# A fixed bound on the deviation, checked by a running minimum, in an attention and squared-ReLU MLP kernel

## The chip, the cores and the metric

The kernel runs on one core of a Trainium2 chip. The metric is the time of one execution on the device in microseconds (us), lower is better. The engines of the core work side by side, each on its own queue in order: TensorE (PE; its weight loads are PEld), VectorE (DVE), ScalarE (ACT), GpSimd (POOL) and SyncE (SP), which issues the DMA transfers.

## The reference

For each of four batches of 12480 tokens with 128 channels, 32 inducing points attend to the tokens, which gives h (32 x 128); then the tokens attend to h; the result goes through an MLP with 2048 hidden columns and a squared ReLU.

```python
def mab(q, kv):
    s = scale * (q @ kv.transpose(0, 2, 1))
    s = s - s.max(-1, keepdims=True)
    a = np.exp(s)
    a /= a.sum(-1, keepdims=True) + 1e-09
    return a @ kv
h = mab(I, x)                 # I: 32 inducing points, x: (4, 12480, 128)
y = mab(x, h).reshape(-1, 128)
hid = y @ w_in                # w_in 128 x 2048, w_out 2048 x 128
return np.maximum(hid, 0.0) ** 2 @ w_out
```

## The kernel before

**Data.** x comes twice: transposed as xT (128 channels on the partitions) and as it is, xn. Both weight matrices come as 64-bit floats and are narrowed to 32 bits on VectorE (`narrow`, lines 199 to 212, tiles named ni, no; seven instructions for each of eight pieces of 128 x 512). A batch has 26 chunks of 480 tokens, in seven groups G: six of four chunks and one of two. A group of xT (`xp`, 128 x 1920 f32, 960 KB) serves as many as three readers: the first scores, the maximum described below, and the second scores. Nine such buffers exist. xn is loaded in 14 pieces per batch (`xnb`, five buffers).

**Stages of a batch b.**

- `first(b)`: scores of the inducing points (s, line 236), moved to sT with their maxima (line 254); the overall maximum (mx, m, gm, nb); exponentials on ScalarE (line 300); transposes (en, line 310); h is summed on TensorE from en and xnb (hacc, line 323) and from group to group on VectorE (hq, line 331); scaled and transposed it is hn and hT.
- `prepare(b)`: because the attention of a token over the 32 points of h is nearly uniform, the MLP is expanded about the mean. hwv = h times w_in (line 448). From the largest and smallest entry of each hidden column (hi_c, lo_c) and a bound rho on the relative deviation follows whether the column is always positive, always dead, or mixed. Positive columns are folded into products of pairs of inducing points (G, line 605; wq, line 611; w16), mixed ones, at most 16, get slots of their own. The bound: `largest(G)` in `first` (line 292) takes the largest absolute value of each channel over the tokens of a group (`xm`), 28 reductions in all; `prepare` multiplies it by the largest deviation of h from its mean (dh) on TensorE and gets rho with the maximum row.
- `second(b, G)`: the second scores (s, line 236, with hT), transposed to e, softmax over the 32 points (lines 364 to 375, on VectorE, GpSimd and ScalarE), transposed back (a32), and written as a high and a low 16-bit half of a - 1/32, scaled by 2^14 (a16: line 385 on ScalarE or 387 on VectorE, then the rest at line 388 on VectorE). It goes to DRAM (ad, line 389) and comes back transposed (dT, line 409, `load_dT`).
- `squares(b, G)`: the mixed slots and the rest of the singles (sq, z, zz, back into dT, lines 422 to 434).
- Chunks: `up` makes hp from dT and a constant `pairs` (line 639), `lift` squares it on ScalarE (g, line 648), `down` sums po (lines 654, 655), which is moved to o with scale and bias (line 658 on ScalarE or 660 on VectorE) and stored.

**Order.** `background(k)` deals out the steps of `second`, `squares`, and of `first` and `prepare` of the next batch beside the chunks, so many by each half chunk. `to_act` sends a movable copy (outputs, a16, w16) to whichever of ScalarE and VectorE has less in the running sums `held`, to which every larger step adds its estimated time. The tile context is opened with `schedule_with_timeline_sim=True`: when the program is built, a simulated timeline sets the order of the instructions on every engine, so an edit moves others too.

**Proof at the end.** For each batch `flags` holds whether the mixed columns fit in 16 slots, whether rho is at most 2^-8, and whether the scales fit. Their minimum is read into a register; where it is 0, a second, full path over all columns (`every_column`) runs for all batches.

Of the kernel before, what the change touches and what calls it, by code (L numbers as in the profile page):

```python
# [31 lines left out]
RHO_MAX = 2.0 ** -8  # L32
# [8 lines left out]
def attend_then_relu2_mlp(ctx: ExitStack, tc: tile.TileContext, xn, xT, indT, w_in, w_out, outT):  # L41
# [78 lines left out]
    flags = const.tile([1, NB], F32, name="flags")  # L120
# [119 lines left out]
    def first(b):  # L240
# [49 lines left out]
        def largest(G):  # L290
            held["dve"] += 60 + 1.042 * 4 * WID[G]
            nc.vector.tensor_reduce(  # L292
                st.xm[:, G:G + 1], st.xp[G], axis=AX.X, op=ALU.max, apply_absolute_value=True,
            )

# [11 lines left out]
        for G, nb32 in enumerate(BLK):  # L307
# [7 lines left out]
            largest(G)  # L315
# [121 lines left out]
    def prepare(b):  # L437
# [44 lines left out]
        nc.tensor.matmul(ps[:, 0:2], ones, row, start=True, stop=True)  # L482
        two = small("two", 2)
        nc.vector.tensor_copy(two, ps[:, 0:2])
        rho = two[:, 1:2]
# [15 lines left out]
        ts(omr, rho, -1.0, 1.0, op0=ALU.mult, op1=ALU.add)  # L501
# [438 lines left out]
```

## Time and profile before

| | us |
|---|---|
| three runs: median (lowest to highest) | 562.29 (556.12 to 562.49) |
| the profiled execution | 565.03 |
| its span from first to last instruction | 563.2 |

| engine | busy us | share of the span |
|---|---|---|
| TensorE | 422.6 | 75% |
| VectorE | 365.6 | 65% |
| ScalarE | 294.4 | 52% |
| GpSimd | 82.2 | 15% |

The profile page gives, for one execution, the busy time of each engine, the span in 40 slices of 14.1 us with a digit for the busy tenths, the clock granted to TensorE in tenths, and the share of the 16 DMA engines. A group of instructions (line, engine, operation, result<-operands, count) has its busy time, the mean of one in ns, and behind the bar the idle time before it and who ended it. The chain of work that ended last is followed back from the last instruction, at each step to what released it. HBM reads are 64.91 MB and writes 31.95 MB over the span.

### The profile page before, as it was taken

To read this page: it belongs to the slowest core of one execution; us is meant where nothing else is said; L and a number is where in the kernel's file an instruction comes from. 1 tells how busy PE (TensorE), PEld (TensorE's weight loads), DVE (VectorE), ACT (ScalarE), POOL (GpSimd) and SP (SyncE) were. 2 spreads that over 40 slices of the span, in tenths; PEclk is the share of its full clock that TensorE was granted. 3 is DMA by queue.
4 is the path that set the end of the run, shared out by engine and by line. 5 is a ranking of instruction groups with operands and counts; after the bars stand their busy time and mean duration, and the time that the engine had idled before them with its cause. 6 is when DMAs were issued, how large, how long until landed. Compare 5 with 4: busy or idle time off the path is not lost.

```text
span 563.2 us, 8828 instructions
## 1 busy us (share of the span) xinstructions
PE 422.6 (75%) x3083; PEld 202.7 (36%) x3083; DVE 365.6 (65%) x947; ACT 294.4 (52%) x419; POOL 82.2 (15%) x93
## 2 busy tenths in 40 slices
PE   1635355986778988869789889779779989669792
PEld 0023334622233535522244536423234555223340
DVE  8999768466382674675574384986653377787541
ACT  0030113338395794334687883426486875357771
POOL 0000011021120110122211010132121021234200
PEclk9999557699697998776899988878898999898987
DMA  8998313126559863253778943263567312244642
GB/s 317 410 358 310 132 70 118 41 80 212 140 160 345 292 216 115 72 169 107 216 237 294 334 167 115 76 227 115 174 216 264 128 54 72 90 151 133 203 150 82
DMA packets 64591, 100.83 MB, mean 179 GB/s; under 512 B 22800, under 2 KB 53776, under 8 KB 64528
## 3 DMA queue, kind: packets, MB, share of 16 engines
q1 hardware_dynamic: 64528, 100.08, 52.9%
q8 instruction: 28, 0.46, 0.4%
q14 instruction: 35, 0.29, 0.2%
HBM read 64.91 MB, written 31.95 MB: 172 GB/s over the span
## 4 chain that ended last, share of the span: by engine, by line
PE 39%; DMA 24%; DVE 22%; ACT 5%; SPq 4%; issue 3%; POOL 0%; ACTq 0%; DVEq 0%; POOLq 0%
PE hp L639 11%; DMA dT<-ad 7%; PE po L654 6%; PE s L236 6%; DMA xp_False<-xT_dram 6%; DMA ad<-a 5%; DVE xm L292 5%; ACT g L648 4%; DMA xnb<-xn_dram 3%; PE wq L611 3%; DVE G L605 3%; PE hwv L448 3%; PE hacc L323 2%; SPq L409 2%; DMA outT_dram<-o 2%
## 5 line engine op out<-in xcount | busy, mean ns | idle before, releaser
L648 ACT ACTIVATE g<-hp 128x960 f16<-128x960 f32 x208 | 193.5, 972 | 105.0 <-PE hp L639 92.8
L639 PE MATMUL hp<-dT,pairs 96*128 96x480 f16 x416 | 129.3, 407 | 16.2 <-ACT g L648 9.6
L654 PE MATMUL po<-g,w 128*128 128x480 f16 x416 | 114.7, 381 | 13.0 <-DVE o L660 5.1
L639 PEld LDWEIGHTS <-pairs 96*128 96x128 f16 x416 | 36.8, 104 | 84.4 <-issue 60.2
L368 POOL TENSOR_TENSOR e<-e,mx 128x480 f32<-128x480 f32 (+1 forms) x28 | 27.0, 965 | 261.5 <-DVE mx L364 208.2
L654 PEld LDWEIGHTS <-w 128*128 128x128 f16 x416 | 40.9, 102 | 63.6 <-issue 24.6
L292 DVE TENSOR_REDUCE xm<-xp_False 128x1 f32<-128x1920 f32 (+1 forms) x28 | 55.9, 1999 | 8.4 <-DMA xp_False<-xT_dram 8.3
L658 ACT ACTIVATE o<-po,bias,osc 128x480 f32<-128x480 f32 x66 | 48.7, 757 | 15.6 <-PE po L655 14.7
L236 PE MATMUL s<-xp_False,indT_sb 128*32 128x480 f32 (+1 forms) x224 | 37.4, 756 | 18.3 <-DMA xp_False<-xT_dram 13.3
L323 PE MATMUL hacc<-xnb,en 128*32 128x128 f32 x784 | 35.6, 317 | 19.6 <-DMA xnb<-xn_dram 7.6
L655 PE MATMUL po<-dT,lin 128*128 128x480 f16 x104 | 39.9, 400 | 9.3 <-DMA dT<-zz 9.0
L432 POOL TENSOR_TENSOR zz<-z 128x480 f16<-128x480 f32 (+1 forms) x28 | 27.6, 985 | 111.7 <-DVE z L428 87.9
L660 DVE TENSOR_SCALAR o<-po,osc,bias 128x480 f32<-128x480 f32 x38 | 28.8, 763 | 18.4 <-PE po L655 13.7
L375 POOL TENSOR_TENSOR e<-e,z 128x480 f32<-128x480 f32 (+1 forms) x28 | 26.9, 961 | 87.8 <-DVE z L374 67.6
L323 PEld LDWEIGHTS hacc<-xnb,en 128*32 128x32 f32 x784 | 25.5, 125 | 32.5 <-issue 15.7
L300 ACT ACTIVATE sT<-sT,nb 128x480 f32<-128x480 f32 (+1 forms) x28 | 18.3, 657 | 35.2 <-DVE nb L287 35.2
L362 DVE STREAM_TRANSPOSE e<-s 128x480 f32<-128x480 f32 (+1 forms) x28 | 18.0, 644 | 25.6 <-PE s L236 25.4
L428 DVE TENSOR_SCALAR z<-sq,off,cut 128x480 f32<-128x480 f32 (+1 forms) x28 | 21.5, 769 | 18.0 <-PE sq L422 17.5
L236 PE MATMUL s<-xp_False,hT 128*32 128x480 f32 (+1 forms) x224 | 30.0, 610 | 0.1
L605 DVE TENSOR_TENSOR G<-hwp,hw 128x512 f16<-128x512 f16 x64 | 25.9, 460 | 5.6 <-PE wq L611 5.6
L378 DVE STREAM_TRANSPOSE a<-e 128x480 f32<-128x480 f32 (+1 forms) x28 | 17.7, 633 | 13.0 <-POOL e L375 13.0
L422 PE MATMUL sq<-dT,singles 96*32 96x480 f16 x104 | 11.4, 398 | 19.4 <-DMA dT<-ad 18.0
(208 smaller groups left out, 493.3 us busy)
## 6 DMA issues: line engine op xcount, KB each, us to landing
outT_dram<-o SPq DMA_DIRECT2D x104, 240.0 KB, 2.6
xp_False<-xT_dram SPq DMA_DIRECT2D x24, 960.0 KB, 6.3
xnb<-xn_dram SPq DMA_DIRECT2D x28, 448.0 KB, 5.8
xnb<-xn_dram SPq DMA_DIRECT2D x24, 512.0 KB, 6.5
dT<-ad SPq DMA_DIRECT2D x72, 120.0 KB, 2.6
ad<-a SPq DMA_DIRECT2D x24, 240.0 KB, 2.6
dT<-zz SPq DMA_DIRECT2D x104, 30.0 KB, 1.9
wi<-w_in_dram SPq DMA_DIRECT2D x4, 512.0 KB, 5.7
```

The lines of the kernel that those rows point to most:

```text
L236: nc.tensor.matmul(ps[32 * q:32 * q + 32, 0:w], lhsT, xp[:, w * q:w * q + w], start=True, stop=True,)
L292: nc.vector.tensor_reduce(st.xm[:, G:G + 1], st.xp[G], axis=AX.X, op=ALU.max, apply_absolute_value=True,)
L323: st.last = nc.tensor.matmul(hacc[32 * q:32 * q + 32, 0:P], en[:, t], xg[:, t % 8], start=t < 4, stop=t + 4 >= nb32,)
L368: nc.gpsimd.tensor_tensor(e[:, 0:t], e[:, 0:t], mx[:, 0:t].unsqueeze(2).broadcast_to([P, t, MI]), op=ALU.subtract)
L432: nc.gpsimd.tensor_tensor(g[rows], zv[rows], zv[rows], op=ALU.mult)
L605: tt(g[:, :, MI * j:MI * j + n], hwp[:, :, 0:n], hw16f[:, :, s0:s0 + n], op=ALU.mult)
L639: nc.tensor.matmul(hp[:, i, 0:CH].rearrange("p (q t) -> p q t", q=4), pairs[0:96, (2 * j + i) * P:(2 * j + i + 1) * P], self.dT[0:96], sta ...
L648: nc.scalar.activation(self.g[:, 2 * j:2 * j + 2], self.hp.pop(j)[:, 0:2, 0:CH], AF.Square)
L654: nc.tensor.matmul(po[:, 0:CH], st.w16[:, i], self.g[:, i], start=i == 0, stop=False)
L655: nc.tensor.matmul(po[:, 0:CH].rearrange("p (q t) -> p q t", q=4), st.lin, self.dT, start=False, stop=True)
L658: nc.scalar.activation(o, po[:, 0:CH], AF.Identity, bias=st.bias, scale=st.osc)
L660: nc.vector.tensor_scalar(o, po[:, 0:CH], st.osc, st.bias, op0=ALU.mult, op1=ALU.add)
```

## The change

The bound on the deviation is no longer computed from the data but fixed at 2^-10 (RHO) and checked afterwards. `largest`, its tile xm, and the instructions of `prepare` that make rho of it (dh, ah, the product of xm and dh, the second half of row, omr, the second flag) are gone; the columns' classes use the constant. In `second`, a running minimum over all tokens, `least_d` (128 x 480, 16 bits), takes in each high half of a16 just after the low half; `smallest()`, one step behind the last `second`, reduces it, transposes it on TensorE, reduces again and compares it with -0.498, which goes into a fifth flag. Since `largest` no longer adds to `held`, the balance of `to_act` shifts: output evictions on ScalarE and VectorE are 40 and 64 instead of 66 and 38, a16 conversions 13 and 15 instead of 19 and 9, w16 14 and 2 instead of 16 and 0. The simulated timeline then orders every queue anew.

```diff
-RHO_MAX = 2.0 ** -8
+RHO = 2.0 ** -10
+D_MIN = -0.498
...
-    flags = const.tile([1, NB], F32, name="flags")
+    flags = const.tile([1, NB + 1], F32, name="flags")
+    least_d = const.tile([P, CH], F16, name="least_d")
+    nc.vector.memset(least_d, 0.0)
...
-        def largest(G):
-            held["dve"] += 60 + 1.042 * 4 * WID[G]
-            nc.vector.tensor_reduce(
-                st.xm[:, G:G + 1], st.xp[G], axis=AX.X, op=ALU.max, apply_absolute_value=True,
-            )
-
...
             if G + 2 < NG:
                 exp(G + 2)
-            largest(G)
...
         if not again:
+            nc.vector.tensor_tensor(least_d[:, 0:w], least_d[:, 0:w], a16[:, 0, 0:w], op=ALU.min)
             st.aT[G] = load_dT(b, G)
...
-            if h == 0:
-
-                xm, dh, ah = small("xm"), small("dh", MI), small("ah", MI)
-                nc.vector.tensor_reduce(xm, st.xm, axis=AX.X, op=ALU.max)
-                ts(dh, st.hT[:, 0:MI], st.hT[:, P:P + 1], None, op0=ALU.subtract)
-                stt(dh, dh, -1.0, dh, op0=ALU.mult, op1=ALU.max)
-                stt(ah, st.hT[:, 0:MI], -1.0, st.hT[:, 0:MI], op0=ALU.mult, op1=ALU.max)
-                stt(dh, ah, 2.0 ** -18, dh, op0=ALU.mult, op1=ALU.add)
...
-        nc.tensor.matmul(ps[0:1, P:P + MI], xm, dh, start=True, stop=True)
-        row = work.tile([1, 2], F32, tag="row", name=f"row_{b}")
-        nc.vector.tensor_reduce(row[:, 0:1], ps[0:1, 0:P], axis=AX.X, op=ALU.max)
-        nc.vector.tensor_reduce(row[:, 1:2], ps[0:1, P:P + MI], axis=AX.X, op=ALU.max)
-        ts(row[:, 0:1], row[:, 0:1], 2.0 ** -60, None, op0=ALU.max)
-        ts(row[:, 1:2], row[:, 1:2], 2 * scale * (1 + 2.0 ** -8), 2.0 ** -16, op0=ALU.mult, op1=ALU.add)
+        row = work.tile([1, 1], F32, tag="row", name=f"row_{b}")
+        nc.vector.tensor_reduce(row, ps[0:1, 0:P], axis=AX.X, op=ALU.max)
+        ts(row, row, 2.0 ** -60, None, op0=ALU.max)
...
-        ts(vm, v, omr, None, op0=ALU.mult)
-        ts(up, hi, 0.0, rho, op0=ALU.max, op1=ALU.mult)
+        ts(vm, v, 1.0 - RHO, None, op0=ALU.mult)
+        ts(up, hi, 0.0, RHO, op0=ALU.max, op1=ALU.mult)
...
-        ts(fits[:, 0:1], bp[0:1, 2:3], MX + 0.5, None, op0=ALU.is_le)
-        ts(fits[:, 1:2], row[:, 1:2], RHO_MAX, None, op0=ALU.is_le)
-        tt(flags[:, b:b + 1], fits[:, 0:1], fits[:, 1:2], op=ALU.mult)
+        ts(flags[:, b:b + 1], bp[0:1, 2:3], MX + 0.5, None, op0=ALU.is_le)
...
+    def smallest():
+
+        m = small("dmin")
+        nc.vector.tensor_reduce(m, least_d, axis=AX.X, op=ALU.min)
+        tp = att_psum("dmin_t")
+        nc.tensor.transpose(tp[0:1, 0:P], m, ident)
+        t = work.tile([1, 1], F32, tag="dmin1", name="dmin1")
+        nc.vector.tensor_reduce(t, tp[0:1, 0:P], axis=AX.X, op=ALU.min)
+        nc.vector.tensor_scalar(flags[:, NB:NB + 1], t, D_MIN, None, op0=ALU.is_ge)
+        yield
+
+    ahead = chain(*(second(b, G) for b in range(NB) for G in range(NG)), smallest())
```

The line numbers of the kernel after are some lower or higher than before: sT is line 254 before and 256 after, narrow 206 to 212 and 208 to 214, `second`'s lines 362 to 388 become 357 to 383, and line 386 is the new minimum.

The first place is VectorE's queue in the first scores of batch 0, where the scores s are moved to sT between the steps of narrowing w_in (ni) and, before, the maxima (xm). Before:

```order
L254 TENSOR_SCALAR sT_213,mx_215<-s_0_2_238 128x480
L292 TENSOR_REDUCE xm_133<-xp_3_False 128x1
L208 TENSOR_SCALAR ni_m<-ni_a 128x512
L254 TENSOR_SCALAR sT_213,mx_215<-s_0_3_254 128x480
L292 TENSOR_REDUCE xm_133<-xp_4_False 128x1
L254 TENSOR_SCALAR sT_213,mx_215<-s_0_4_260 128x480
L209 SCALAR_TENSOR_TENSOR ni_r<-wi_175,ni_m 128x512
L292 TENSOR_REDUCE xm_133<-xp_5_False 128x1
L292 TENSOR_REDUCE xm_133<-xp_6_False 128x1
L254 TENSOR_SCALAR sT_213,mx_215<-s_0_5_274 128x480
```

After:

```order
L256 TENSOR_SCALAR sT_213,mx_215<-s_0_2_238 128x480
L210 TENSOR_SCALAR ni_m<-ni_a 128x512
L211 SCALAR_TENSOR_TENSOR ni_r<-wi_177,ni_m 128x512
L212 TENSOR_TENSOR ni_r<-ni_a,ni_r 128x512
L213 TENSOR_SCALAR ni_m<-wi_177 128x512
L256 TENSOR_SCALAR sT_213,mx_215<-s_0_3_254 128x480
L214 SCALAR_TENSOR_TENSOR w_in_sb<-ni_m,ni_r 128x512
L256 TENSOR_SCALAR sT_213,mx_215<-s_0_4_260 128x480
L256 TENSOR_SCALAR sT_213,mx_215<-s_0_5_274 128x480
L208 TENSOR_SCALAR no_a<-wo_266 128x512
```

The narrowing has moved up to where the maxima were: the last piece of w_in is done here, and the first of w_out (wo) begins.

The second place is VectorE's queue at the end of batch 0's `first`, from the scaling of h (zr, hn) to hT and the scale of w_out (wo_m). Before:

```order
L338 TENSOR_SCALAR zr<-hs_502 128x1
L212 SCALAR_TENSOR_TENSOR wo_sb<-no_m,no_r 128x512
L207 SCALAR_TENSOR_TENSOR no_a<-wo_272,no_a 128x512
L339 RECIPROCAL zr<-zr 128x1
L686 TENSOR_REDUCE wm_170<-wo_sb 128x1
L208 TENSOR_SCALAR no_m<-no_a 128x512
L340 TENSOR_SCALAR hn_134<-hs_502,zr 128x128
L209 SCALAR_TENSOR_TENSOR no_r<-wo_272,no_m 128x512
L344 COPY hT_155<-ht_508 128x128
L345 TENSOR_REDUCE hT_155<-ht_508 128x1
L210 TENSOR_TENSOR no_r<-no_a,no_r 128x512
L211 TENSOR_SCALAR no_m<-wo_272 128x512
```

After:

```order
L333 TENSOR_SCALAR zr<-hs_495 128x1
L334 RECIPROCAL zr<-zr 128x1
L335 TENSOR_SCALAR hn_135<-hs_495,zr 128x128
L339 COPY hT_155<-ht_501 128x128
L340 TENSOR_REDUCE hT_155<-ht_501 128x1
L187 TENSOR_REDUCE wo_m<-wo_t 1x1
L341 TENSOR_SCALAR hT_155<-hT_155 128x1
L188 TENSOR_SCALAR wo_m<-wo_m 1x1
```

The narrowing of the last piece of w_out (wo_272) now stands ahead of the third group's sum hq, before the last transposes en, and no longer between the small steps.

The third place is VectorE's queue where batch 1 takes over from batch 0: the last products G_1_3 for wq, and the attention weights of batch 1's second group (z2_1_1, a32_1_1, a16_1_1), whose result goes to ad and dT. Before:

```order
L372 TENSOR_REDUCE z2_1_1_2071<-e2_1_1_1971 128x15
L292 TENSOR_REDUCE xm0_133<-xp_2_3_False_2321 128x1
L373 TENSOR_SCALAR z2_1_1_2071<-z2_1_1_2071 128x15
L605 TENSOR_TENSOR G_1_3_2051<-hwp_1_1745,hw16_1_1697 128x16x32 x3
L605 TENSOR_TENSOR G_1_3_2051<-hwp_1_1745,hw16_1_1697 128x16x16
L607 CAST G_1_3_2051<-hwS_1_1740 128x16x16
L613 TENSOR_REDUCE wm5_1918<-wq_1_2_2028 128x1
L374 RECIPROCAL z2_1_1_2071<-z2_1_1_2071 128x15
L378 STREAM_TRANSPOSE a32_1_1_2122<-e2_1_1_1971 128x480
L388 SCALAR_TENSOR_TENSOR a16_1_1_2124<-a32_1_1_2122,lessen_105,a16_1_1_2124 128x480
```

After:

```order
L368 TENSOR_SCALAR z2_1_1_2029<-z2_1_1_2029 128x15
L591 TENSOR_REDUCE wm5_1876<-wq_1_2_1986 128x1
L369 RECIPROCAL z2_1_1_2029<-z2_1_1_2029 128x15
L638 TENSOR_SCALAR o_0_24_2146<-po_0_24_2140,osc0_142,bias0_143 128x480
L373 STREAM_TRANSPOSE a32_1_1_2080<-e2_1_1_1929 128x480
L591 TENSOR_REDUCE wm5_1876<-wq_1_3_2034 128x1
L638 TENSOR_SCALAR o_0_25_2187<-po_0_25_2181,osc0_142,bias0_143 128x480
L594 TENSOR_REDUCE cm2_1826<-wm5_1876 128x1
L383 SCALAR_TENSOR_TENSOR a16_1_1_2082<-a32_1_1_2080,lessen_105,a16_1_1_2082 128x480
L386 TENSOR_TENSOR least_d_133<-least_d_133,a16_1_1_2082 128x480
```

The maximum ahead of z2 is gone; two outputs of batch 0 (o_0_24, o_0_25), which ScalarE moved before, stand between the reciprocal and a16, and the minimum behind it.

More of the change, by code (lines that the diff above doesn't have):

```diff
@@ L127, in attend_then_relu2_mlp @@
         one = Batch()
-        one.xm = const.tile([P, NG], F32, name=f"xm{k}")
         one.hn = const.tile([P, P], F32, name=f"hn{k}")
@@ L473, in prepare @@
         nc.tensor.transpose(ps[0:1, 0:P], am, ident)
-        nc.tensor.matmul(ps[0:1, P:P + MI], xm, dh, start=True, stop=True)
-        row = work.tile([1, 2], F32, tag="row", name=f"row_{b}")
-        nc.vector.tensor_reduce(row[:, 0:1], ps[0:1, 0:P], axis=AX.X, op=ALU.max)
-        nc.vector.tensor_reduce(row[:, 1:2], ps[0:1, P:P + MI], axis=AX.X, op=ALU.max)
-        ts(row[:, 0:1], row[:, 0:1], 2.0 ** -60, None, op0=ALU.max)
-        ts(row[:, 1:2], row[:, 1:2], 2 * scale * (1 + 2.0 ** -8), 2.0 ** -16, op0=ALU.mult, op1=ALU.add)
+        row = work.tile([1, 1], F32, tag="row", name=f"row_{b}")
+        nc.vector.tensor_reduce(row, ps[0:1, 0:P], axis=AX.X, op=ALU.max)
+        ts(row, row, 2.0 ** -60, None, op0=ALU.max)
         yield
         ps = att_psum(f"bc_{b}")
[L482 to L485, printed above, removed]
+        nc.tensor.matmul(ps[:, 0:1], ones, row, start=True, stop=True)
         p2 = small("p2")
-        ts(p2.bitcast(I32), two[:, 0:1].bitcast(I32), 0x7F800000, None, op0=ALU.bitwise_and)
-        mg, nmg, s, k2, omr = small("mg"), small("nmg"), small("s"), small("k2"), small("omr")
+        ts(p2.bitcast(I32), ps[:, 0:1].bitcast(I32), 0x7F800000, None, op0=ALU.bitwise_and)
+        mg, nmg, s, k2 = small("mg"), small("nmg"), small("s"), small("k2")
         ts(k2, p2, 2.0, None, op0=ALU.mult)
@@ L500, in prepare @@
         ts(nmg, p2, -2.0 ** -16, None, op0=ALU.mult)
-        ts(omr, rho, -1.0, 1.0, op0=ALU.mult, op1=ALU.add)
         up, dn, dead, pos, mix, inc = (small(n, NF) for n in ("up_c", "dn_c", "dead", "pos", "mix", "inc"))
         vm = small("vm", NF)
-        ts(vm, v, omr, None, op0=ALU.mult)
-        ts(up, hi, 0.0, rho, op0=ALU.max, op1=ALU.mult)
+        ts(vm, v, 1.0 - RHO, None, op0=ALU.mult)
+        ts(up, hi, 0.0, RHO, op0=ALU.max, op1=ALU.mult)
         tt(up, up, vm, op=ALU.add)
@@ L508, in prepare @@
         stt(dead, up, nmg, dead, op0=ALU.is_le, op1=ALU.max)
-        ts(dn, lo, 0.0, rho, op0=ALU.min, op1=ALU.mult)
+        ts(dn, lo, 0.0, RHO, op0=ALU.min, op1=ALU.mult)
         tt(dn, dn, vm, op=ALU.add)
@@ L545, in prepare @@
         stt(inc, inc, pl, mix, op0=ALU.add, op1=ALU.mult)
-        fits = work.tile([1, 2], F32, tag="fits", name=f"fits_{b}")
-        ts(fits[:, 0:1], bp[0:1, 2:3], MX + 0.5, None, op0=ALU.is_le)
-        ts(fits[:, 1:2], row[:, 1:2], RHO_MAX, None, op0=ALU.is_le)
-        tt(flags[:, b:b + 1], fits[:, 0:1], fits[:, 1:2], op=ALU.mult)
+        ts(flags[:, b:b + 1], bp[0:1, 2:3], MX + 0.5, None, op0=ALU.is_le)
         hot = flow.tile([P, NF, MX], F32, tag="hot", name=f"hot_{b}", bufs=1)
@@ L703, in attend_then_relu2_mlp @@
     N_SECOND, N_SCORES, N_HEADS, N_PRE, N_SQ = 4, 2 * NG, 20, 23, 2
-    ahead = chain(*(second(b, G) for b in range(NB) for G in range(NG)))
+    def smallest():
[8 more added lines that the diff above has]
+    ahead = chain(*(second(b, G) for b in range(NB) for G in range(NG)), smallest())
     sqs = chain(*(squares(b, G) for b in range(NB) for G in range(NG)))
@@ L723, in background @@
         b, c = k // (2 * NCH), k % (2 * NCH) / 2.0
-        give("ahead", ahead, min(math.ceil((NG * b + c / 4 + min(3, 2 + k / 16)) * N_SECOND), NB * NG * N_SECOND))
+        give("ahead", ahead, min(math.ceil((NG * b + c / 4 + min(3, 2 + k / 16)) * N_SECOND), NB * NG * N_SECOND + 1))
         if b + 1 < NB:
```

## The prediction

> **What bounds the kernel now.** I read the page first (busy time and slices), then the chain of work that ended last in order of time, then the timeline of the places where the removed instruction stands in that chain.
>
> ```profile
> PE 422.6 (75%) x3083; PEld 202.7 (36%) x3083; DVE 365.6 (65%) x947; ACT 294.4 (52%) x419; POOL 82.2 (15%) x93
> ...
> PE   1635355986778988869789889779779989669792
> ...
> DVE  8999768466382674675574384986653377787541
> ...
> PEclk9999557699697998776899988878898999898987
> DMA  8998313126559863253778943263567312244642
> ```
>
> No engine is full, TensorE least idle (75%). But the first four digits of DVE and DMA are 9 and 8 to 9 while PE stands at 1 to 6: the first 56 us are set by VectorE and the input loads. The clock row falls to 5 right behind that.
>
> ```profile
> 12.23 2.15 DVE xm L292
> ...
> 46.22 2.03 DVE xm L292
> ...
> 95.09 0.97 PE hp L639 x4
> ```
>
> In the chain (start, length, what) the maximum over xp, `xm`, stands eight times (nine instructions) between 12 and 48 us, together 17.6 us (first and last shown), and once more at 77; behind that it goes through the round trip of the attention weights over DRAM (a16 to ad, ad to dT) to the first hp at 95. So the reduce lies on the path of the start. The timeline shows how (start, length, engine, instruction, in brackets what the engine waited for).
>
> ```profile
> 3.06 5.93 SPq L231 DMA_DIRECT2D xp_False<-xT_dram  x7
> ...
> 28.37 1.03 PE L236 MATMUL s<-xp_False,indT_sb 128*32 128x240 f32 x8 [0.81 <-DVE sT L254]
> ...
> 37.19 0.70 ACT L300 ACTIVATE sT<-sT,nb 128x480 f32<-128x480 f32 x1 [35.16 <-DVE nb L287]
> ...
> 55.31 0.64 PE L323 MATMUL hacc<-xnb,en 128*32 128x128 f32 x16 [0.65 <-DMA xnb<-xn_dram]
> ...
> 57.93 0.28 DVE L331 TENSOR_TENSOR hq<-hacc,hq 128x128 f32<-128x128 f32 x1
> 58.13 0.68 DVE L210 TENSOR_TENSOR no_r<-no_a,no_r 128x512 f32<-128x512 f32 x1
> 58.27 0.80 PE L336 MATMUL hs<-hq,rep 128*128 128x129 f32 x2 [2.31 <-DVE hq L331]
> ...
> 64.79 0.68 DVE L686 TENSOR_REDUCE wm<-wo_sb 128x1 f32<-128x512 f32 x1
> ...
> 66.72 0.58 PE L189 MATMUL wo_b<-wo_m,ones 1*128 1x1 f32 x2 [0.55 <-DVE wo_m L186]
> ...
> 67.23 3.62 PE L448 MATMUL hwv<-hT,w_in_sb 128*128 128x33 f32 x16
> ...
> 77.10 2.15 DVE L292 TENSOR_REDUCE xm<-xp_False 128x1 f32<-128x1920 f32 x1 [0.64 <-DMA xp_False<-xT_dram]
> 79.17 0.68 DVE L463 TENSOR_REDUCE hi_c<-hwv 128x16 f32<-128x512 f32 x1
> ```
>
> Before the start is over VectorE does three things in one queue: xm, the narrowing of the two weight matrices, and the small steps of attention. The last score at 28.37 waits for VectorE, the exponentials start at 37.19, and the last xn arrives when it is wanted (0.65 of wait at 55.31).
>
> ```profile
> 0.00:40.00 40.00, 13.81 (x79) 2.96 (x83) 37.18 (x94) 4.10 (x10) 1.18 (x9) 1.00 0.97 375
> 40.00:44.00 4.00, 2.76 (x48) 1.95 (x40) 3.96 (x7) 1.85 (x7) 0.00 (x0) 1.00 0.60 174
> ...
> 98.00:540.00 442.00, 365.82 (x2668) 172.14 (x2669) 274.71 (x717) 269.02 (x381) 76.07 (x79) 0.88 0.52 167
> ```
>
> Busy time by stretch: VectorE is busy 37.18 of the first 40 us and 3.96 of the next 4. DMA is full for 40 us (375 GB/s, 15.0 MB) and then idles: 0.60 of 40 to 44, since five xnb buffers wait for hacc. In the long middle (98 to 540) VectorE and ScalarE are both about 62% busy, TensorE 83%, at clock 0.88.
>
> **The change, step by step**, against the profiled execution's own 565.03 us (span 563.2, and 1.8 around it), which lies 2.7 above the median of 562.29 of the three runs shown.
>
> ```profile
> L292 DVE TENSOR_REDUCE xm<-xp_False 128x1 f32<-128x1920 f32 (+1 forms) x28 | 55.9, 1999 | 8.4 <-DMA xp_False<-xT_dram 8.3
> L658 ACT ACTIVATE o<-po,bias,osc 128x480 f32<-128x480 f32 x66 | 48.7, 757 | 15.6 <-PE po L655 14.7 <-ACT o L658 0.7 <-ACT g L648 0.2
> ...
> L660 DVE TENSOR_SCALAR o<-po,osc,bias 128x480 f32<-128x480 f32 x38 | 28.8, 763 | 18.4 <-PE po L655 13.7 <-DMA outT_dram<-o 4.6
> ...
> L605 DVE TENSOR_TENSOR G<-hwp,hw 128x512 f16<-128x512 f16 x64 | 25.9, 460 | 5.6 <-PE wq L611 5.6
> ...
> L210 DVE TENSOR_TENSOR no_r<-no_a,no_r 128x512 f32<-128x512 f32 x4 | 2.7, 683 | 0.0
> ```
>
> Removed are the 28 xm of 55.9 us, 11 of them before 98 us, and a dozen small instructions per batch. Added are 28 minima on 16-bit tiles of 480: by the nearest row with two 16-bit sources and a 16-bit result (L605, 512 wide) 0.46 each, 12.9 in all; by the f32 row L210 at most 0.68, 19.1 in all. I take 0.46, the same types. Since xm no longer counts in the balance of `to_act`, 26 output evictions (66 to 40 on ScalarE), six a16 conversions and two of w16 move to VectorE: 26 x 0.757 = 19.7 off ScalarE and 26 x 0.763 = 19.8 onto VectorE, and eight smaller ones, no dearer than these, so at most 6 more on each side. So behind the start VectorE loses 17 xm (34), gains some 23 of these and 24 minima (11): there it is no lighter, only without its 2.1 us blocks.
>
> *Start, scores.* The loads don't change place:
>
> ```profile
> xp_False<-xT_dram SPq DMA_DIRECT2D x1, 480.0 KB, 16.3
> ```
>
> The seventh xp is issued near 9.0 (3.06 + 5.93) and takes 16.3: 25 us. Its scores take 1.03, so 26.4 with handover, and the new order leaves some 4.2 us of VectorE between them and the exponentials (six of the seven instructions of one conversion, 3.1, and five small ones): 30.6 for 37.19.
>
> *Start, accumulation.* From 37.19 to the last hq (58.2) VectorE worked 20.9 us without a break. Two xm (4.3), the rest of w_in (1.1) and the 3.1 already done go; the twelve conversion instructions from 58.13 to 64.79 (first and last shown, 7.1 in all) now stand ahead: 20.9 - 4.3 - 1.1 - 3.1 + 7.1 = 19.5, so 50.1, and two groups of hacc and their sums behind the last transposes, about 2.2: 52.3. The loads allow it: 3.9 MB of xn are left at 40 us, and at 375 GB/s they land by 50.4.
>
> *Start, to hwv.* From 58.2 to 67.23 went 9.0 us; without the conversion's 7.1 VectorE has 1.9 left, and TensorE's hs and wo_b take 1.4, two transposes and the handovers some 0.9: 4.2, hwv at 56.5. That is 10.7 earlier.
>
> *Prepare.* At 77.10 xm, which itself let VectorE wait 0.64 for its load, stands ahead of hi_c: 2.1 to 2.8, I take 2.5. The small chain from am to hws is shorter too, but the first a16, not hws, starts the round trip: nothing taken. The start is worth 13.2; its bounds are 8 (only the loads' 5 and this 2.5, conversions still in the way) and 19.8 (every xm of the chain up to 79).
>
> *Middle.* Four xm are in the chain there.
>
> ```profile
> 135.04 2.15 DVE L292 TENSOR_REDUCE xm<-xp_False 128x1 f32<-128x1920 f32 x1 [1.43 <-DMA xp_False<-xT_dram]
> ...
> 144.41 0.59 PE L422 MATMUL sq<-dT,singles 96*32 96x480 f16 x4 [4.45 <-DMA dT<-ad]
> ```
>
> At 135.04 VectorE waits 1.43 for the load and is then busy 2.15, ahead of the subtractions of two a16; ad and dT start late, and TensorE waits 4.45 for dT.
>
> ```profile
> 135.04 0.83 DVE xm L292
> ...
> 153.43 1.15 DVE xm L292
> ...
> 238.39 2.06 DVE xm L292
> ...
> 249.07 5.13 DMA dT<-ad
> ...
> 361.36 2.06 DVE xm L292
> ```
>
> The chain's pieces of xm are 0.83 (at 135), 1.15 (at 153), 2.06 and 2.06. At 238 two evictions (o_0_24, o_0_25) now stand where xm stood, so I count 1.0 there: 5.0 in all. Bounds: 0, where another wait takes over, and 6.1.
>
> ```profile
> PE hp L639 <- ACT g L648: 9.6, 19, 1.2
> ...
> PE po L654 <- DVE o L660: 5.1, 4, 2.1
> ```
>
> ScalarE's relief: TensorE waits 9.6 for g; I take 2 of it. The moved evictions: TensorE waited 5.1 for 38 on VectorE; for 64 that is 8.6, 3.5 more; about half of it, +1.8, since an eviction on ScalarE delays g, and so TensorE, too. The minimum stands behind the subtraction whose result starts ad, so it delays only the next instruction, at about three places of the chain: +1.5. The final proof (reduce, transpose, reduce, compare) runs with the last second(), beside some ten chunks of MLP; without that cover about 1.5 us.
>
> Sum: -13.2 - 5.0 - 2.0 + 1.8 + 1.5 = -16.9, so 548.1 for the profiled execution and 545.4 for the median.
>
> [...] What a gap of TensorE costs afterwards:
>
> ```profile
> 141.00:144.00 3.00, 0.00 (x0) 0.00 (x0) 0.00 (x0) 0.00 (x0) 0.00 (x0) 0.50 0.99 263
> ...
> 147.00:150.00 3.00, 3.00 (x16) 0.76 (x18) 0.34 (x2) 1.83 (x2) 0.00 (x0) 0.50 0.14 31
> ```
>
> Behind the gap of 4.45 us the granted clock is 0.50 for nine us, and TensorE works 5.6 of them at half speed. My sum counts each us of a shorter gap once. [...]
>
> **The rivals.** A change within 2% (about 11 us, 551 to 574) is what a measurement of this kernel can hardly tell from none.
>
> *Start limited, middle empty.* The conversions or the loads take the place of xm at the start (8), and the middle loses nothing because the queues were ordered anew and TensorE waits for other transfers: 562.3 - 8 = 554. For it: DMA at 0.97 over 40 us, and VectorE full without xm until 50. Against it: the hole of 0.60 at 40 to 44.
>
> *Gaps close.* Three gaps behind an xm (135, 238, 361) get short enough for the clock to stay up: three times half of 5.6, and 4 of the start's cold work: 545 - 12 = 533. For it: the row of 0.50. Against it: the gap behind 238 holds a dT of 5.13 that nothing here shortens. [...]
>
> *Slower.* An eviction on VectorE waits for TensorE's po, or for one of the three o buffers, and everything behind it in VectorE's queue waits too: the next batch's a16 come late and TensorE runs dry. It decides from 17 us of the sum above, 26 x 0.65 each; for 2% slower it needs 28, 26 x 1.1, and gives 574. Against it: 38 such evictions cost TensorE 5.1 in all, 0.13 each.
>
> *The bound doesn't hold.* Where the proof fails, the whole second path runs, and the time is far above all this. The least a16 allowed is -0.498 in units of 2^-14; by the scales of the inputs the scores of one token differ between inducing points by a few 10^-5, times 2^14 / 32 = 512 that is 0.01 to 0.1 in that unit. Two in 100, counted with the slower case.
>
> **How the numbers follow.** Forecast (start 10 to 16, middle 0 to 8 faster: 538 to 551): 0.52. Start limited, 551 to 557: 0.26. Gaps close, 528 to 538: 0.15. Slower, with the failed proof: 0.07. The time is the forecast's, 545. From 531 to 557 leaves out part of the third case (0.06) and the last (0.07), and a little between. Faster by over 2% (below 551): 0.52 + 0.15 + 0.02 from the edge of the second = 0.69; slower 0.07; within 0.24.
>
> **What would show it.** Exponentials near 31 instead of 37, the last hq near 52, hwv near 56, first hp near 82 instead of 95: the start. If hq is at 55 and waits for xnb, the loads took over; if it waits for nothing, the conversions. L660 with x64, near 0.76 each, and waits of TensorE for it near 9 us; above 20 the slower case holds. The minimum at 0.40 to 0.50; at 0.68 the other bound. In the middle, the sum of TensorE's idle time between 85 and 527 of 71 or less instead of 76 (442 - 366), and a clock above 0.88 if gaps close. The forecast is wrong where the start gains less than 8, or the middle gets longer by more than 5.

## The result, and the profile after

| | before | after |
|---|---|---|
| median (lowest to highest), us | 562.39 (556.12 to 564.34, 4 runs) | 525.55 (522.30 to 528.55, 4 runs) |
| the profiled execution, its span | 565.03, 563.2 | 528.31, 526.5 |

The ratio is 0.936, interval 0.926 to 0.947: faster by 6.4%, 36.8 us. The forecast was 545, from 531 to 557; the time lies below that range. Measured again on another chip, the kernel after stands at 0.946 of before, 28.6 us faster (see below).

The page of the kernel after: busy time of the engines, then four rows of the 40 slices (13.2 us each now).

```profile
PE 408.7 (78%) x3076; PEld 198.4 (38%) x3076; DVE 344.0 (65%) x941; ACT 274.7 (52%) x385; POOL 83.0 (16%) x93
...
PE   1645839788778889667979979678989888769991
...
DVE  8897385563724287974735275987853577987841
...
PEclk9956558989979799979979789899989889798997
DMA  8999532076679754556479733278496021245652
```

VectorE's share of the span is still 65%. TensorE does only 7 matmuls fewer but is busy 14 us less, 10.8 of it in the middle of the run, where the granted clock is 0.92 and was 0.89 (below). The clock row has its 5s and 6s in slices 3 to 6 and stands at 7 to 9 behind them; before, 5s and 6s come as late as slice 19.

The chain of the kernel after through the start (start, length, what):

```profile
29.55 0.57 PE mb L287 x2
...
34.60 10.16 DMA xnb<-xn_dram
44.83 4.90 DMA xnb<-xn_dram
...
52.86 0.30 DVE hq L326
...
55.79 0.58 PE wo_b L191 x2
56.38 3.56 PE hwv L444 x16
...
65.69 0.69 DVE hi_c L451
```

The maxima are gone from it and so is the narrowing between hq and hwv. In their place the loads of xn hold the chain from 34.60 to 49.73. The exponentials stand off the chain now, in the timeline:

```profile
30.44 0.69 ACT L296 ACTIVATE sT<-sT,nb 128x480 f32<-128x480 f32 x1 [28.42 <-DVE nb L289]
...
43.47 1.08 PE L318 MATMUL hacc<-xnb,en 128*32 128x128 f32 x14 [5.71 <-DMA xnb<-xn_dram]
```

The groups that the forecast named, and some of the waits of TensorE (us in all, times, longest), in the kernel after:

```profile
L638 DVE TENSOR_SCALAR o<-po,osc,bias 128x480 f32<-128x480 f32 x64 | 48.9, 766 | 28.9 <-PE po L633 17.5
...
L386 DVE TENSOR_TENSOR least_d<-least_d,a 128x480 f16<-128x480 f16 x24 | 10.4, 433 | 0.0
...
L386 DVE TENSOR_TENSOR least_d<-least_d,a 128x240 f16<-128x240 f16 x4 | 1.1, 276 | 0.0
```

```profile
PE hacc L318 <- DMA xnb<-xn_dram: 14.7, 10, 5.7
PE po L633 <- DMA dT<-zz: 14.1, 6, 5.8
...
PE sq L418 <- DMA dT<-ad: 6.9, 6, 1.8
...
PE po L632 <- DVE o L638: 1.7, 2, 1.1
```

So the span divides as follows (places: first hp, the last products of batch 0's wq, last hp, end):

| stretch | before | after | difference | forecast |
|---|---|---|---|---|
| to the first hp | 95.1 | 83.3 | -11.8 | -13.2 |
| to the end of the first wq | 19.6 | 15.0 | -4.6 | 0 |
| the middle, to the last hp | 435.2 | 414.9 | -20.3 | -3.7 |
| end | 13.3 | 13.3 | 0 | 0 |

The start came as forecast. The middle did not; the second stage is taken up again below. Busy time in the middle of before and of after, each row with stretch and length, then busy us and instructions of TensorE, its weight loads, VectorE, ScalarE and GpSimd, and last the granted clock, the DMA share and GB/s:

```profile
114.70:549.90 435.20, 361.04 (x2596) 167.06 (x2597) 271.38 (x688) 273.08 (x383) 77.05 (x80) 0.89 0.53 173
```

```profile
98.30:513.20 414.90, 350.29 (x2591) 164.90 (x2592) 269.23 (x701) 253.18 (x349) 77.61 (x80) 0.92 0.56 181
```

VectorE's work in the middle is the same (271 and 269 us: 17 maxima left, 26 evictions, some conversions and the minima came). TensorE is idle 9.6 us less (74.2 to 64.6), and busy 10.8 less, since busy time times clock is 321 in one and 322 in the other. So about half of the middle's gain is idle time and half the clock.

### The profile page after: what moved, and what is told of

Same layout as the page of the kernel before. It is cut to its first block, busy times and chain, and to the rows that moved or that the text cites. A ratio compares the mean times of both kernels' runs of the same rounds, so it can differ in the third digit from the quotient of the medians.

```text
span 526.5 us, 8780 instructions
## 1 busy us (share of the span) xinstructions
PE 408.7 (78%) x3076; PEld 198.4 (38%) x3076; DVE 344.0 (65%) x941; ACT 274.7 (52%) x385; POOL 83.0 (16%) x93
## 4 chain that ended last, share of the span: by engine, by line
PE 42%; DMA 28%; DVE 14%; ACT 7%; issue 3%; SPq 2%; POOL 1%; ACTq 0%; DVEq 0%; POOLq 0%
PE hp L617 10%; PE po L632 8%; DMA dT<-ad 6%; DMA xnb<-xn_dram 6%; PE s L238 6%; DMA ad<-a 5%; DMA dT<-zz 5%; ACT g L626 4%; PE R L510 4%; DVE G L583 3%; DMA wo<-w_out_dram 3%; PE hacc L318 3%; PE hwv L444 3%; PE po L633 2%; PE wq L589 2%
## 5 line engine op out<-in xcount | busy, mean ns | idle before, releaser
L617 PE MATMUL hp<-dT,pairs 96*128 96x480 f16 x416 | 123.1, 391 | 11.6 <-ACT g L626 8.6
L632 PE MATMUL po<-g,w 128*128 128x480 f16 x416 | 118.2, 386 | 5.6 <-ACT o L636 2.5
L638 DVE TENSOR_SCALAR o<-po,osc,bias 128x480 f32<-128x480 f32 x64 | 48.9, 766 | 28.9 <-PE po L633 17.5
L318 PE MATMUL hacc<-xnb,en 128*32 128x128 f32 x784 | 37.3, 320 | 19.6 <-DMA xnb<-xn_dram 14.7
L633 PE MATMUL po<-dT,lin 128*128 128x480 f16 x104 | 40.3, 401 | 14.1 <-DMA dT<-zz 14.1
L238 PE MATMUL s<-xp_False,indT_sb 128*32 128x480 f32 (+1 forms) x224 | 30.6, 640 | 22.1 <-DMA xp_False<-xT_dram 21.1
L636 ACT ACTIVATE o<-po,bias,osc 128x480 f32<-128x480 f32 x40 | 29.5, 754 | 20.0 <-PE po L633 12.3
L583 DVE TENSOR_TENSOR G<-hwp,hw 128x512 f16<-128x512 f16 x64 | 28.1, 493 | 2.6 <-PE wq L589 2.5
L510 PE MATMUL R<-wo_sb,hwS 128*32 128x128 f32 x128 | 20.4, 336 | 9.1 <-DVE hwS L501 9.1
L364 ACT ACTIVATE e<-e 128x480 f32<-128x480 f32 (+1 forms) x28 | 16.1, 574 | 20.9 <-POOL e L363 20.8
L256 DVE TENSOR_SCALAR_CACHE_REDUCE sT<-s 128x480 f32<-128x480 f32 (+1 forms) x28 | 17.2, 615 | 12.4 <-PE s L238 11.8
```

What stands on the lines that cost most here:

```text
L238: nc.tensor.matmul(ps[32 * q:32 * q + 32, 0:w], lhsT, xp[:, w * q:w * q + w], start=True, stop=True,)
L318: st.last = nc.tensor.matmul(hacc[32 * q:32 * q + 32, 0:P], en[:, t], xg[:, t % 8], start=t < 4, stop=t + 4 >= nb32,)
L510: nc.tensor.matmul(ps[0:MI, 0:P], hwS[:, k], wo_sb[:, k], start=k == 0, stop=k == NF - 1)
L583: tt(g[:, :, MI * j:MI * j + n], hwp[:, :, 0:n], hw16f[:, :, s0:s0 + n], op=ALU.mult)
L617: nc.tensor.matmul(hp[:, i, 0:CH].rearrange("p (q t) -> p q t", q=4), pairs[0:96, (2 * j + i) * P:(2 * j + i + 1) * P], self.dT[0:96], sta ...
L632: nc.tensor.matmul(po[:, 0:CH], st.w16[:, i], self.g[:, i], start=i == 0, stop=False)
```

## The experiments

The kernel before ran beside each group of kernels on the same chip (medians 556.5 to 558.8 there). The middle is always the stretch from the last products of batch 0's wq to the last hp; in some kernels it is counted from the start of the last 16 of them, in others from their end, which makes 1.1 us. It is that of the profiled execution, which can lie some us off the median.

| kernel | ratio to before (interval) | middle, us | VectorE | ScalarE | TensorE, clock, product |
|---|---|---|---|---|---|
| before | 1 | 435.2 | 271.4 | 273.1 | 361.0, 0.89, 321 |
| before, nudged | 1.013 (1.006 to 1.020) | 433.0 | 271.8 | 273.7 | 359.1, 0.90, 323 |
| balance only | 0.997 (0.991 to 1.002) | 430.3 | 290.5 | 253.1 | 359.2, 0.90, 323 |
| load of 2 us put back | 0.955 (0.949 to 0.961) | 422.8 | 285.9 | 273.6 | 349.9, 0.90, 315 |
| attention kept | 0.961 (0.948 to 0.974) | 418.1 | 267.8 | 257.9 | 352.8, 0.91, 321 |
| start only | 0.965 (0.956 to 0.974) | 415.8 | 270.3 | 274.0 | 347.6, 0.91, 316 |
| after | 0.936 and 0.946 | 414.9 | 269.2 | 253.2 | 350.3, 0.92, 322 |
| load of 1 us put back | 0.933 (0.924 to 0.943) | 408.4 | 268.8 | 273.7 | 344.6, 0.92, 317 |
| outputs kept | 0.930 (0.921 to 0.940) | 403.1 | 249.9 | 269.4 | 342.9, 0.94, 322 |
| more on ScalarE | 0.929 (0.924 to 0.935) | 402.4 | 229.1 | 292.5 | 341.6, 0.94, 321 |
| the wait alone | 0.926 (0.921 to 0.931) | 401.5 | 249.0 | 273.6 | 338.0, 0.94, 318 |
| no minimum | 0.925 (0.919 to 0.931) | 396.9 | 237.9 | 273.6 | 336.4, 0.94, 316 |
| balance kept, nudged | 0.926 (0.919 to 0.933) | 396.9 | 246.9 | 274.0 | 336.1, 0.94, 316 |
| balance kept | 0.919 (0.910 to 0.928) | 394.4 | 246.3 | 273.5 | 337.1, 0.95, 320 |
| middle only | 0.929 (0.921 to 0.937) | 394.3 | 240.0 | 273.4 | 339.6, 0.94, 319 |

In what follows "balance kept" is the kernel after with one line put back; "start only" and "middle only" are the kernel before with part of its maxima left out. For the maxima that they leave out, their tile holds 0.55 or the values of an earlier batch, so that rho is bounded over the remaining tokens only.

**Balance kept.** The first theory was that the moved evictions had helped.

```diff
@@ first(b), kernel after
+            held["dve"] += 60 + 1.042 * 4 * WID[G]
```

> The kernel after, but the estimated time of the removed maximum still counts in the running sums, so ScalarE keeps its 66 output evictions; no maximum is computed. If the middle's 20 us come from the evictions moved off ScalarE (theory balance), this run lies near 545 (525.5 plus 20). If they come from the maximum no longer standing in VectorE's queue (theory blocks), it lies near 525. If they come from the queues being ordered anew (theory order), anywhere from 520 to 545, and the stages change one by one without a common sign.

510.56 us: 15 faster than the kernel after, below all that was expected. With 66 evictions on ScalarE as before, the middle takes 394.4:

```profile
99.80:494.20 394.40, 337.09 (x2583) 160.43 (x2581) 246.32 (x666) 273.52 (x383) 78.03 (x80) 0.95 0.60 191
```

So the shift of the balance costs time, and the gain has to come from elsewhere. Two executions of the kernel after have 414.9 and 410.8 us in the middle, two of this one 394.4 and 395.8.

**Start only, middle only, balance only.** All from the kernel before: the maxima left out in batch 0, left out in batches 1 to 3, and the line with `held` left out while all maxima stay.

```diff
@@ largest(G): start only (middle only: "if b == 0")
+            if b:
                 nc.vector.tensor_reduce(
...
@@ largest(G): balance only
-            held["dve"] += 60 + 1.042 * 4 * WID[G]
```

> The kernel before, with the maximum left out in batch 0 alone (its result is a constant 0.55, batches 1 to 3 compute theirs; the running sums still count all). Seven of the 11 maxima of the start go. If the start is worth what the trace shows (12 us to the first hp), this lies at 550 to 553; theories balance and blocks both expect no gain behind that. Below 545 would speak for order.

> The kernel before, with the maximum left out in batches 1 to 3 (constant 0.55 or the value of an earlier batch; the running sums still count all). Theory blocks expects the middle's 20 us and the 4 us of the start that belong to batch 1: 538 to 542. Theory balance expects only the start's part, 556 to 560. Theory order: no telling, 540 to 565.

> The kernel before with all 28 maxima, but their estimated time no longer counts in the running sums, so evictions move to VectorE as in the kernel after. Theory balance expects some 20 us less, 542, or somewhat more since VectorE is now fuller by 25 us than in the kernel after; theory blocks expects no gain or a loss, 560 to 570, since VectorE's queue gets longer with the maxima still in it.

535.67, 514.38 and 555.56, beside 556.5 of before. Start only gained 21, of which 9.8 stand ahead of the first hp (85.3); its middle shrank too (435.2 to 415.8), though all its maxima there are kept. That is below the 545 that was set beforehand as the sign of the queues' new order, so a new order may be worth more than the nudges below show. Middle only gained 42 and lies far below the 538 to 542 expected; 6.5 of it are gone by the first hp (88.6) and 11.1 by the last products of the first wq (103.6). So 31 to 36 us belong to the middle by the medians, 40.9 by the profiled executions.

```profile
103.60:497.90 394.30, 339.64 (x2596) 160.50 (x2597) 240.04 (x669) 273.42 (x383) 77.52 (x80) 0.94 0.60 191
```

VectorE is 31.4 us lighter there than in the kernel before, and the middle is shorter by as much or more, although VectorE was busy only 62% of it. Balance only gained nothing: with the maxima in place, the shift neither helps nor hurts.

**How much does another order alone make?** 28 one-column memsets with no reader were put behind `largest`, in the kernel before, and at the same place in the one with the balance kept; the simulated timeline orders all queues anew for them.

```diff
@@ first(b)
+            nc.vector.memset(idle, 0.0)
```

> The kernel before with all its maxima, and beside each a clear of one column (0.1 us or less, 28 times) that nobody reads: work as before, but the queues are ordered anew. Theory load (what VectorE has to do in the middle sets its length, whatever the order) expects the time of before within 1%, ratio 0.99 to 1.01. Theory order expects it to move by 2 to 4% either way.

> The kernel of e1_balance_kept (no maxima, balance as before) with the same idle clears. Theory load: 510 on the scale of e1, within 1% (ratio to before 0.91 to 0.93). Theory order: off by 2 to 4% either way.

564.63 and 515.08: 1.3% and 0.7% slower, little more than the 1% that was expected if the order means nothing. Differences of some 5 us between two kernels are therefore no evidence of a cause. One nudge in each of two kernels doesn't bound what another order can do: start only moved more.

**The load put back without the wait.** In the kernel with the balance kept, a maximum over four copies of the sT group just written, in batches 1 to 3. It needs no transfer and has no reader; only VectorE's time comes back.

```diff
@@ first's scores, behind the copy to sT (half load: [P, 2, w])
+            if b:
+                nc.vector.tensor_reduce(
+                    idle, sT[:, 480 * G:480 * G + w].unsqueeze(1).broadcast_to([P, 4, w]), axis=AX.X, op=ALU.max, apply_absolute_value=True,
+                )
```

> The kernel of e1_balance_kept, and in batches 1 to 3 VectorE reduces the just written 480 scores four times over (1920 elements, the size of the maximum, 21 times, about 2 us each), a result that nobody reads; it needs no load of xp. Theory load expects the middle's gain to go: 21 x 2 us of VectorE make 35 to 42 us, ratio to before 0.985 to 1.0. If the maximum hurt by waiting for the load of xp in front of VectorE's queue, and not by its length, most of the gain stays: ratio 0.92 to 0.94.

533.10, 0.955, between the two expectations: some 20 us of time came back with 42 us of VectorE (18 of 2.14 and 3 of 1.15), and not all that leaving out the maxima had gained. One of them can be followed in the timeline of this kernel (start, length, engine, instruction, the wait ahead):

```profile
117.07 2.14 DVE L261 TENSOR_REDUCE idle<-sT 128x4 f32<-128x1920 f32 x1
...
119.13 0.17 DVE L374 TENSOR_SCALAR z<-z 128x15 f32<-128x15 f32 x1
119.33 0.25 DVE L375 RECIPROCAL z<-z 128x15 f32<-128x15 f32 x1
...
119.72 0.99 POOL L376 TENSOR_TENSOR e<-e,z 128x480 f32<-128x480 f32 x1 [1.43 <-DVE z L375]
...
132.75 0.59 PE L424 MATMUL sq<-dT,singles 96*32 96x480 f16 x4 [6.69 <-DMA dT<-ad]
```

The sums z stand behind the block for 2 us, GpSimd's product waits for z, and at the end of that round trip TensorE stands still for 6.69 us. The block isn't the only cause of this gap: the chain that ended last runs, just ahead of it, through ScalarE's conversion of a16 and not through the block:

```profile
124.84 0.59 ACT a L386
...
126.53 2.51 DMA ad<-a
...
129.92 2.79 DMA dT<-ad
```

In the kernel with the balance kept, the wait at this place is 1.34:

```profile
124.67 0.39 PE L419 MATMUL sq<-dT,singles 96*32 96x480 f16 x4 [1.34 <-DMA dT<-ad]
```

Over the whole run the products sq wait for this transfer 25.9 us with the load and 11.0 without it (18.0 in the kernel before). This one wait isn't a measure of the rest: it is 6.9 in the kernel after and 7.8 with half the load, while the transfer behind it (zz to dT) makes TensorE wait 14.1 and 17.2 there, and 7.7 to 9.0 in the other three. All waits for dT together are 33.3 in the kernel before, 36.3 with the load, 25.0 with half of it, 23.8 in the kernel after and 20.3 with the balance kept. And the gap is paid again afterwards, in the stretches behind it:

```profile
129.00:132.00 3.00, 0.00 (x0) 0.00 (x0) 0.00 (x0) 0.00 (x0) 0.00 (x0) 0.50 0.88 237
132.00:135.00 3.00, 2.25 (x13) 0.47 (x14) 0.78 (x1) 0.00 (x0) 0.69 (x1) 0.50 0.45 107
135.00:138.00 3.00, 3.00 (x12) 0.70 (x15) 2.82 (x3) 1.83 (x2) 0.30 (x1) 0.50 0.10 21
138.00:141.00 3.00, 3.00 (x21) 1.08 (x14) 2.27 (x5) 1.11 (x2) 0.21 (x1) 0.91 0.57 160
```

TensorE works from 132.75 at half clock for over 5 us (0.91 in the last row is half a us more of it), doing 12 matmuls in a stretch that holds 21 afterwards. Between 118 and 133 the kernel with the balance kept shows a clock of 1.00.

> The kernel with the kept sum and, in batches 1 to 3, a maximum over two copies of sT, about 1 us, where four copies (2 us, 21 times) had brought 0.955 of before from 0.92, 18 to 20 us. If the time goes with the length of VectorE's work: about half, 0.935 to 0.94 (520 to 524 us). If only long blocks of 2 us delay the round trip: 0.92 to 0.925 (512 to 515 us). If the mere presence of an instruction at that place orders the queue anew: near 0.955 (532 us).

519.45, about 8 us, for half the load, as expected if the time goes with the length of VectorE's work. It is little more than the 5 us of a nudge; what it excludes is that an instruction at that place costs 20 us whatever its length.

**More on ScalarE, the wait alone, no minimum.** All from the kernel with the balance kept: its line doubled (o 89 on ScalarE, 15 on VectorE); a copy of one column of xp where the maximum stood, so that VectorE waits for the transfer again without the work; the running minimum left out, and with it the proof over the tokens.

```diff
@@ more on ScalarE
-            held["dve"] += 60 + 1.042 * 4 * WID[G]
+            held["dve"] += 120 + 1.042 * 8 * WID[G]
@@ the wait alone
+            if b:
+                nc.vector.tensor_copy(idle, st.xp[G][:, 0:1])
@@ no minimum
-            nc.vector.tensor_tensor(least_d[:, 0:w], least_d[:, 0:w], a16[:, 0, 0:w], op=ALU.min)
```

> The kernel of e1_balance_kept with twice the phantom time in the running sums: 89 of 104 output evictions and 26 of 28 a16 conversions on ScalarE instead of 66 and 19, so VectorE has some 20 us less still and ScalarE 20 more. Theory load expects a further gain of 10 to 20 us (ratio 0.885 to 0.90) unless ScalarE becomes the bound; if the two are balanced in e1 already, 0.92 or above.

> The kernel of e1_balance_kept, and in batches 1 to 3 VectorE copies one column of each xp (0.1 us, 21 times, a result that nobody reads) where the maximum stood: it has to wait for the load of xp like the maximum, but takes no time. If the wait for the load in VectorE's queue was part of the maximum's price, the time rises by 5 to 15 us (ratio 0.93 to 0.945); if only its length counted, the ratio stays 0.915 to 0.926.

> The kernel of e1_balance_kept without the running minimum (28 instructions of some 0.4 us on VectorE; the final check reads the cleared tile, so the proof over the tokens is left out). By theory load, 0.5 to 0.7 us of time per us of VectorE in the middle, 24 x 0.4 x 0.6 = 6 us less: ratio 0.905 to 0.915. If it is hidden, 0.915 to 0.926.

518.03, 516.81 and 514.54. More relief of VectorE (229 us in the middle) gains nothing further; ScalarE stands at 292 us then. Whether it takes over as the limit was not shown. With the wait alone VectorE stood 11.7 us in all before these copies (8.3 before the maxima of the kernel before), and the kernel is 4 us slower, as much as by an idle nudge, so it stays undecided whether the wait costs anything. Without the minimum the kernel is no faster, although 6 us were expected for 8 us less of VectorE: no cost of the minimum is seen, and the time doesn't simply go with VectorE's total.

**The two again, on one chip:**

> The kernel after, unchanged, for a comparison on one chip with the next. Expected: ratio to before 0.93 to 0.945.

> The kernel of e1_balance_kept again, on the same chip as the kernel after. If keeping the 26 evictions on ScalarE is worth something beyond the 1% that a new order alone moves, it is 1.5 to 3% faster than the kernel after (ratio to before 0.91 to 0.925); if not, they lie within 1%.

528.08 for the kernel after (0.946, 0.940 to 0.952), 512.68 with the balance kept (0.920, 0.914 to 0.925): the difference is 15 us, 2.9%, and the second is the fastest kernel of this study.

**Which of the moved instructions?** The kernel after with the places of the movable copies written in as lists: the outputs as in the kernel with the balance kept, the conversions of a16 and w16 as in the kernel after; and the reverse.

```diff
-    def to_act(act, dve):
+    def to_act(act, dve, kind=""):
+        if fixed.get(kind):
+            return fixed[kind].pop(0) == "1"
...
```

> The kernel after, with the 66 output evictions on ScalarE that the kept sum gave, but the a16 and w16 conversions where the kernel after has them (13 of 28 and 14 of 16 on ScalarE); the places are written into the code as lists. The kernel with the kept sum stands at 0.92 of before, the kernel after at 0.936 and 0.946. If the outputs on VectorE carry the cost of the shift: 0.92 to 0.925 (512 to 515 us). If the a16 conversions on VectorE carry it, since they stand in the round trip: 0.936 to 0.946 (522 to 527 us). Between them: both.

> The other half: the a16 and w16 conversions where the kept sum puts them (19 of 28 and 16 of 16 on ScalarE), the output evictions as in the kernel after (40 on ScalarE, 64 on VectorE). If the a16 conversions carry the cost: 0.92 to 0.925 (512 to 515 us). If the outputs do: 0.936 to 0.946 (522 to 527 us). If both this and the run with the outputs kept stand near 0.94, neither alone explains it and the order that comes with each set is as likely a cause.

517.27 with the outputs kept, 533.55 with only the conversions kept; the intervals in the table are wide. The first lies 5 us above the kernel with the balance kept, the second 5 us above the kernel after, each as much as a nudge. So the 26 output evictions carry most of the cost of the shift. The conversions, though they stand in the round trip, carry none that these runs show.

## Why the prediction was wrong

**Start, scores; accumulation; to hwv; prepare: right.** Forecast and measured: exponentials 30.6 and 30.44, end of the last hq 52.3 and 53.2, hwv 56.5 and 56.38, first hp about 82 and 83.3. The path of the accumulation is another than the one that the forecast added up: TensorE waits for xnb (5.71 at 43.47), and the chain runs over the loads up to 49.73. The forecast had the two close together, VectorE done at 50.1 and the loads at 50.4, so that it came out right on either. The rival in which only 8 us are left falls. The forecast had the stretch behind, from the first hp to the last products of wq, at nothing, and it became shorter by 4.6. There the granted clock is 1.00 after and 0.74 before:

```profile
95.10:114.70 19.60, 16.64 (x131) 10.79 (x131) 10.75 (x47) 7.47 (x11) 0.00 (x0) 0.74 0.11 32
```

```profile
83.30:98.30 15.00, 11.97 (x129) 7.33 (x127) 9.13 (x43) 6.94 (x10) 0.00 (x0) 1.00 0.12 32
```

That is no work of the change. The same stretch of the kernel after in its second execution, and of "balance only", which has all maxima, are the other way round:

```profile
81.76:100.86 19.10, 16.61 (x129) 10.45 (x128) 9.52 (x45) 7.01 (x10) 0.00 (x0) 0.73 0.12 33
```

```profile
94.20:110.10 15.90, 12.25 (x133) 8.03 (x133) 10.78 (x47) 7.40 (x11) 0.14 (x1) 1.00 0.14 40
```

So the 4.6 us are the luck of where the clock stood, and nothing was the right term.

**Middle, 5.0 from the chain's pieces of xm: the step that failed.** The maxima of the middle were worth 31 to 36 us by the medians of the run without them (40.9 by the profiled executions), at least six times the term. The chain names, at each moment, one releaser; it showed four of 17 maxima, where they were the last cause. That the others delayed the round trip as well, beside another cause of like size, fits the runs but wasn't followed one by one. What the runs show: work that is put into VectorE's queue ahead of the attention weights lengthens the middle. From the kernel with the balance kept, 22.5 us more of it make the middle 14 longer, and 39.6 more make it 28 longer, 0.6 to 0.7 for each us; by the medians, which lie 4 to 5 below those two profiled executions, it is 0.3 to 0.5. With the full load, idle time of TensorE grew by 15.7 (57.3 to 73.0) and its busy time, with the clock at 0.90 instead of 0.95, by 12.8; the sum counted each us of a gap once.

**Relief of ScalarE (-2.0) and moved evictions (+1.8): wrong in size.** Together they were forecast at nothing; the runs have them at +15 by the medians, and +15.0 and +20.5 by two pairs of profiled executions. The count and the price were right (64 of 766 ns). The cost is not where the forecast looked: TensorE's own wait for these evictions, which it put at 8.6 us, is 1.7 in the kernel after. They make VectorE 23 us longer in the middle (246 to 269), but that doesn't explain all: the half load adds as much to VectorE and costs half as much time by the medians. The slower rival names a second cause, that VectorE waits for po or for an o buffer with everything behind it. In the kernel after it stands 28.9 us before these evictions, with the balance kept 12.5:

```profile
L639 DVE TENSOR_SCALAR o<-po,osc,bias 128x480 f32<-128x480 f32 x38 | 29.1, 767 | 12.5 <-PE po L634 9.7 <-DMA outT_dram<-o 1.6 <-PE hp L618 0.7
```

No run separates these waits from the length. The rival's price, from 17 us on, was near; the time fell all the same because the maxima were worth more.

**Minimum, +1.5: no cost found.** It measured 0.43 us, near the 0.46 taken, and its removal gains nothing.

So the sum for the middle should have read about -31 + 15 + 0 = -16, or with the other bound -36 + 15 = -21, by the medians, and -41 + 20.5 = -20.5 by the profiled executions, in place of -3.7; -20.3 was measured. The medians of the repeat fit this: 28.6 us in all, some 12 of them at the start. The 36.8 of the first measurement stand beside a kernel before of 562.39. The two errors have opposite signs, and with the balance kept the time would have been 15 us lower still. Of the rivals "gaps close" at 533 (528 to 538) came nearest, in time and in kind, though the time lies below it too; it counted three gaps where the clock rose in the mean of the whole middle, 0.89 to 0.92. That the clock stays up behind a shorter gap was the author's estimate and was not shown: it fell behind gaps of 2.35 and 1.80 us as well (last section). The forecast's own test, an idle TensorE of 71 or less between 85 and 527, misleads: 78.1 was measured, because the kernel now ends at 526.5 and its last 13.3 us, with TensorE busy for 2.4 of them, lie inside that stretch. Taken in the middle, it is 64.6 for 74.2; the clock, the other half of that test, did rise above 0.88 (0.91 from 85 to 527).

**What stays open.** The kernel before and its nudged form need 433 to 435 us in the middle at 271 to 272 us of VectorE, while start only, after and the half load need 408 to 416 at 269 to 270. The length of VectorE's work doesn't tell these apart, nor why "balance only", with 290 us of it, needs no more than before. Part may be the order, for which the nudges show 5 us and start only speaks for more; part the profiled execution of before, which at 565 lies 6 to 8 above the medians of the other chips; the wait for xp made about 4. Nor is it known why the shift of the balance costs 15 us without the maxima and nothing with them.

## What to carry to other kernels

An engine that is 62% busy can still set the time, where its queue feeds a round trip that TensorE waits for: price a removal there by taking it out, and not by its share of the chain that ended last. A harmless load of the same length, put back, shows whether length alone does it; here it brought back about two thirds. When work leaves an engine, look at every heuristic that counted it: here one line of bookkeeping, left out along with the work, gave 15 of the gained us back. Where a simulated timeline orders the queues, measure first what an idle instruction does to the time, since 1% can come from the order alone. And profile a kernel twice before a stage is credited to the change: a stretch of 15 us took 19 in another execution, at a granted clock of 0.73 instead of 1.00.

## What the runs showed of the hardware

Not expected was how much of the time is the clock: over the fifteen kernels of the table TensorE's busy time in the middle runs from 336 to 361 us, and times the granted clock it is always 315 to 323. From the kernel before to the kernel after the middle has 9.6 us less of idle TensorE and 10.8 less of busy; with the load of 2 us put back, 15.7 more and 12.8 more. By these two pairs, as an estimate, a shorter wait is paid back about twice.

Not expected either was how short a gap goes with a fall of the clock. The prediction saw the half clock behind the gap of 4.45 us. In the kernel before the clock falls as that gap begins (139.96), and ahead of it lies one of 2.35:

```profile
138.79 0.97 PE L654 MATMUL po<-g,w 128*128 128x480 f16 x4 [2.35 <-ACT o L658]
```

```profile
139.00:140.00 1.00, 0.97 (x5) 0.29 (x3) 0.00 (x0) 0.39 (x1) 0.00 (x0) 0.96 0.92 301
140.00:141.00 1.00, 0.00 (x0) 0.00 (x0) 0.00 (x0) 0.75 (x1) 0.00 (x0) 0.50 1.10 400
```

In the kernel after it falls just before 147, behind a gap of 1.80:

```profile
146.34 0.56 PE L617 MATMUL hp<-dT,pairs 96*128 96x480 f16 x2 [1.80 <-ACT g L626]
```

```profile
147.00:148.00 1.00, 1.00 (x4) 0.43 (x3) 0.23 (x1) 1.00 (x3) 0.00 (x0) 0.50 0.34 59
```

So these gaps of 2.35 and 1.80 us, both shorter than 4.45, didn't keep the clock up. The half clock then lasts through over 5 us of TensorE's work: from 132.75 on with the load of 2 us put back, and for 5.6 us in the kernel before. The whole stretch at half clock, idle time included, is about 10.2 us in both, 128.3 to 138.5 and 139.9 to 150.2, and 6.8 in the kernel after, 146.9 to 153.7.
